# Loading two groups of an output projection's rows in five parts of unequal partition counts, in a one-core decode kernel

## The chip, the core and the metric

The kernel runs on one core of a Trainium2 chip. Its time is the device time of one execution in microseconds (us). It was run three times: 2528.84, 2529.17 and 2529.18 us, median 2529.17 us. A separate execution was profiled; the profile's times count from its first instruction.

## What is computed

One token passes through two branches that are mixed by a gate. Branch A is attention over a cache of 65,536 positions with 32 heads of 128; branch B is a small feed-forward network. All inputs are bf16.

```python
def _A_ref(x, k_cache, v_cache, wq, wo):          # x [1,1,512], caches [1,32,65536,128]
    q = (x @ wq).reshape(B, Sq, H, Dh).transpose(0, 2, 1, 3)
    scores = jnp.einsum("bhqd,bhkd->bhqk", q, k_cache) * (Dh ** -0.5)
    p = _softmax(scores, axis=-1)
    o = jnp.einsum("bhqk,bhkd->bhqd", p, v_cache)
    return o.transpose(0, 2, 1, 3).reshape(B, Sq, H * Dh) @ wo      # wo [4096,512]

def _B_ref(x, w_gate, w_up, w_down):
    return (_silu(x @ w_gate) * (x @ w_up)) @ w_down

g = _sigmoid((x * gate_w).sum(-1, keepdims=True))
return g * _A_ref(...) + (1 - g) * _B_ref(...)
```

The two caches are 512 MiB each, so the kernel reads some 1,088 MB and computes little on each byte.

## The kernel before, in words

**Tiles.** A head's 65,536 positions are cut into four tiles of 16,384 positions (G = 4). A tile is a [128 partitions x 16,384] bf16 block of 4 MB, loaded by one DMA from SyncE's queue (SP, line 112), 32 KB contiguous to a partition. There are 128 K tiles and 128 V tiles. They share a ring of five slots of 4 MB (SLOTS, lines 78 to 89): `take` draws the next free slot, `give` puts it back after the last reader.

**A K tile** is multiplied by the head's query on VectorE (line 245), halved by additions (line 249), and summed by matmuls with an identity into PSUM (`scores`, line 258); `fold` (line 272) reduces the result to one score a position. After the fourth tile of a head come the maximum (`row_max`), the exponentials (`exponentials`) and their total.

**A V tile** is multiplied by the exponentials in 32 matmuls (`values`, line 313). After a head's fourth V tile, `head_copy` and `head_turn` turn the result into a column of 128 values, and `project` (line 356) multiplies it with the head's 128 rows of wo.

**wo** comes in two ways. The first 16 heads use small tiles of four heads each (WG = 4), from a pool of two buffers (`wo_pool`, line 69), loaded by `load_wo` (line 158): one DMA of 128 partitions, four heads, 512 numbers, that is four separate rows of 1 KB to a partition, 512 KB in all. The last 16 heads' rows (`wo_late`) are loaded at the very end into a ring slot, in four pieces (`load_late`, line 163).

**The order of work** is written out by hand. Each step of the main loop (line 408) takes one K tile n and one V tile v: it issues the load of K tile n, then, at every sixteenth V tile (v = 2, 18, 34, 50), a group of wo, then the load of V tile v; after that come the vector work, the matmuls and the projection of a head that is done. All these loads are issued by SP, in this order, and a load waits until its slot's last reader is through. The built program gives each load one of eight landing semaphores in turn.

**The end.** The last three V tiles are loaded in pieces (V_CUTS, line 30), the smallest of 256 KB, then `wo_late`; then the last head is turned, 16 heads are projected, the two halves of the sum are copied (lines 459 and 460) and the output of 1 KB is stored (line 461).

Of the kernel before, what the change touches and what calls it, by code (L numbers as in the profile page):

```python
# [11 lines left out]
P = 128  # L12
# [14 lines left out]
LATE = 16  # L27
LATE_CUTS = (0, 5, 10, 14, LATE)
TURNED = 8
V_CUTS = {3: (0, 64, NB), 2: (0, 64, NB), 1: (0, 32, 64, 96, 112, NB - TURNED, NB)}  # L30


@with_exitstack
def kernel(
# [14 lines left out]
    nc = tc.nc  # L49
# [56 lines left out]
    def load(dst, cache, n, name, cuts=(0, NB)):  # L106
        h, g = divmod(n, G)
        t = take(f"{name}.{n}")
        view = t.rearrange("p (j d) -> p j d", d=Dh)
        src = cache[0, h, g * NB * P : (g + 1) * NB * P, :].rearrange("(p j) d -> p j d", j=NB)  # L110
        for a, b in zip(cuts[:-1], cuts[1:]):
            nc.sync.dma_start(out=view[:, a:b, :], in_=src[:, a:b, :])
        dst[n] = view
# [4 lines left out]
    def load_v(n):  # L118
        load(V_tiles, A_v_cache, n, "V_t", V_CUTS.get(N - n, (0, NB)))

# [35 lines left out]
    wo_tiles = {}  # L156

    def load_wo(g):
        wo_tiles[g] = wo_pool.tile([P, WG, D], bf16, name="wo_sb", tag="wo_sb")
        rows = A_wo[g * WG * P : (g + 1) * WG * P, :]  # L160
        nc.sync.dma_start(out=wo_tiles[g], in_=rows.rearrange("(h p) n -> p h n", p=P))

    def load_late(cuts):
        late = take("wo_late.0")[:, : LATE * D].rearrange("p (h n) -> p h n", n=D)
# [142 lines left out]
    def values(n):  # L307
        h, g = divmod(n, G)
        if g == 0:
            O_tiles[h] = psum_o.tile([4, 4 * Dh], f32, name="O_ps")  # L310
        end = NB if n < N - 1 else NB - TURNED
        for j in range(0, end, 4):
# [16 lines left out]
    def head_turn(h, O_sb):  # L329
        oh_ps = psum_m.tile([P, 1], f32, name="oh_ps", tag="misc")  # L330
        turned = range(NB - TURNED, NB) if h == H - 1 else ()
        for j in turned:
# [75 lines left out]
    for n, v in steps:  # L408
        if n is not None and n > G:
            load_k(n)  # L410
        if v is not None:
            if v % (WG * G) == 2 and v // (WG * G) < (H - LATE) // WG:
                load_wo(v // (WG * G))
            if v:
                load_v(v)
            if v == N - 1:
                wo_late = load_late(LATE_CUTS)
# [74 lines left out]
```

## Time and profile before

| What | Value |
|---|---|
| Median of three runs | 2529.17 us |
| Profiled execution: its own time | 2529.15 us |
| Profiled execution: span from first to last instruction | 2527.4 us |
| DMA packets, bytes | 43,019 packets, 1088.49 MB, mean 431 GB/s |
| K tiles, one load each | 128 of 4096 KB, 36.9 us from issue to landing (median) |
| V tiles in one load | 125 of 4096 KB, 29.2 us from issue to landing (median) |
| wo groups | 4 of 512 KB, 33.8 us from issue to landing (median) |
| SP issues of the wo groups | 426 to 438 ns each, first at 92.8 us, last at 1060.5 us |

The page's engines are PE (TensorE matmul), PEld (its weight loads), DVE (VectorE), ACT (ScalarE), POOL (GpSimd) and SP (SyncE, which here issues nearly all loads). L161 is line 161 of the kernel. The DMA rows give what the core's 16 DMA engines moved: a row for each queue, and a mean busy share over the 16. "instruction" queues bring program code. The time to landing runs from an issue on SP to the last of the load's 16 landing records. The chain of work is followed back from the last instruction, at each step to what released it.

### The profile page before, as it was taken

The page shows a single profiled execution, that of the slowest core. Times are in us where ns is not written, and L with a number is a line of the kernel's source. Part 1 is how long each engine was busy: PE and PEld are TensorE (multiplying, and loading weights), DVE is VectorE, ACT ScalarE, POOL GpSimd, SP SyncE. Part 2 cuts the span into 40 slices and gives each one's busy share as a digit, 9 for nine tenths or more (in the row PEclk, how much of TensorE's full clock was granted, in tenths as well). Part 3 has the DMA queues.
Part 4 walks back from the last instruction along what each step waited for, and adds up shares of the span by engine and source line. Part 5 has one row for each costly group of instructions (what it writes and reads, how often), then busy time and mean ns, then how long its engine had stood idle before and what let it go on. Part 6 is the DMA issues. An engine that isn't in the chain of part 4 may idle for free.

```text
span 2527.4 us, 13150 instructions
## 1 busy us (share of the span) xinstructions
PE 1523.3 (60%) x5770; PEld 579.9 (23%) x5770; DVE 2083.6 (82%) x744; ACT 77.6 (3%) x207; POOL 0.7 (0%) x6
## 2 busy tenths in 40 slices
PE   3666556655666555556665666566556665665568
PEld 1322222221222212212222222222222221222223
DVE  6988888788888999988888888888888888888860
ACT  1000000000000000000000000000000000000000
POOL 0000000000000000000000000000000000000000
PEclk7877777777777777787777777777877777777779
DMA  9999999999999999999999999999999999999998
GB/s 415 435 431 431 434 434 432 433 432 431 434 431 435 432 431 433 433 432 434 432 433 432 432 433 434 433 432 432 433 434 433 432 432 432 435 434 432 431 432 370
DMA packets 43019, 1088.49 MB, mean 431 GB/s; under 512 B 4689, under 2 KB 8786, under 8 KB 9170
## 3 DMA queue, kind: packets, MB, share of 16 engines
q1 hardware_dynamic: 42674, 1087.65, 99.9%
q8 instruction: 45, 0.74, 0.1%
q14 instruction: 12, 0.10, 0.0%
q10 hardware_dynamic: 288, 0.00, 0.0%
HBM read 1087.64 MB, written 0.00 MB: 430 GB/s over the span
## 4 chain that ended last, share of the span: by engine, by line
DMA 71%; PE 22%; DVE 6%; issue 0%; ACT 0%; SPq 0%; DVEq 0%
DMA V_t<-in_A_v_cache_dram 65%; PE O_ps L313 21%; DMA K_t<-in_A_k_cache_dram 6%; DVE K_t L245 3%; DVE K_t L249 2%; PE S_ps L258 1%; DMA wo_late<-in_A_wo_dram 0%; DVE S_sb L272 0%; PE oh_ps L342 0%; DVE m L278 0%; ACT P_sb L291 0%; PE a_ps L356 0%; PE mT_ps L282 0%; ACT O_sb L326 0%; DVE top L287 0%
## 5 line engine op out<-in xcount | busy, mean ns | idle before, releaser
L313 PE MATMUL O_ps<-V_t,P_sb 128*4 128x512 bf16 x4094 | 1149.9, 451 | 672.4 <-DMA V_t<-in_A_v_cache_dram 672.4
L245 DVE TENSOR_TENSOR K_t<-K_t,q_bc 128x16384 bf16<-128x16384 bf16 (+1 forms) x159 | 1117.2, 7026 | 346.0 <-DMA K_t<-in_A_k_cache_dram 346.0
L249 DVE TENSOR_TENSOR K_t<-K_t 128x8192 bf16<-128x8192 bf16 (+1 forms) x314 | 859.8, 2738 | 8.6
L313 PEld LDWEIGHTS <-P_sb 128*4 128x4 bf16 x4094 | 392.7, 97 | 1409.4 <-issue 1064.4
L258 PE MATMUL S_ps<-K_t,ident_b 128*128 128x512 bf16 x1056 | 265.3, 395 | 97.3 <-DVE K_t L249 97.1
L258 PEld LDWEIGHTS <-ident_b 128*128 128x128 bf16 x1056 | 98.6, 102 | 245.2 <-issue 156.0
L282 PE MATMUL mT_ps<-diag,ones_f 128*128 128x128 f32 x64 | 23.9, 473 | 141.3 <-ACT diag L280 141.3
L342 PE MATMUL oh_ps<-ident_f,O_sb 4*128 4x1 f32 x256 | 55.5, 334 | 74.5 <-ACT O_sb L326 74.5
L272 DVE TENSOR_REDUCE S_sb<-S_ps 128x128 f32<-128x512 f32 x128 | 87.5, 684 | 4.8 <-PE S_ps L258 4.8
L280 ACT ACTIVATE diag<-ident_f,m 128x128 f32<-128x128 f32 x32 | 12.8, 402 | 2110.1 <-DVE m L278 2110.1
L342 PEld LDWEIGHTS oh_ps<-ident_f,O_sb 4*128 4x128 f32 x256 | 52.8, 301 | 84.1 <-ACT O_sb L326 79.8
L282 PEld LDWEIGHTS mT_ps<-diag,ones_f 128*128 128x128 f32 x64 | 14.9, 289 | 158.4 <-ACT diag L280 158.4
L459 DVE CAST out_sb<-a_ps 1x256 bf16<-1x256 f32 x1 | 0.4, 411 | 58.3 <-PE a_ps L356 58.3
L291 ACT ACTIVATE P_sb<-S_sb,bias 128x512 bf16<-128x512 f32 x32 | 23.1, 722 | 1.0
L278 DVE TENSOR_REDUCE m<-S_sb 128x1 f32<-128x512 f32 x32 | 22.0, 686 | 1.1
L326 ACT ACTIVATE O_sb<-O_ps 4x512 f32<-4x512 f32 x32 | 18.3, 572 | 132.8 <-PE O_ps L313 132.8
L147 PE MATMUL qg_ps<-wq_t,X_bc 128*128 128x512 bf16 x32 | 8.8, 443 | 13.0 <-DMA wq_t<-in_A_wq_dram 13.0
L304 DVE RECIPROCAL recip<-tot_ps 128x1 f32<-128x1 f32 x32 | 5.1, 158 | 12.5 <-PE tot_ps L299 12.5
L299 PEld LDWEIGHTS tot_ps<-rowsum,ones_f 128*128 128x128 f32 x64 | 9.5, 188 | 14.0 <-issue 14.0
L299 PE MATMUL tot_ps<-rowsum,ones_f 128*128 128x1 f32 x64 | 12.2, 260 | 0.0
L349 ACT ACTIVATE oT<-oh_ps,rg 128x1 bf16<-128x1 f32 x32 | 8.4, 264 | 63.4 <-PE oh_ps L342 63.4
L287 DVE TENSOR_REDUCE top<-mT_ps 128x1 f32<-128x128 f32 x32 | 9.1, 284 | 1.0 <-PE mT_ps L282 1.0
(42 smaller groups left out, 68.9 us busy)
## 6 DMA issues: line engine op xcount, KB each, us to landing
K_t<-in_A_k_cache_dram SPq DMA_DIRECT2D x128, 4096.0 KB, 36.9
V_t<-in_A_v_cache_dram SPq DMA_DIRECT2D x125, 4096.0 KB, 29.2
V_t<-in_A_v_cache_dram SPq DMA_DIRECT2D x4, 2048.0 KB, 31.7
wq_t<-in_A_wq_dram SPq DMA_DIRECT2D x1, 4096.0 KB, 12.3
V_t<-in_A_v_cache_dram SPq DMA_DIRECT2D x3, 1024.0 KB, 32.1
wo_sb<-in_A_wo_dram SPq DMA_DIRECT2D x4, 512.0 KB, 33.8
gu_t<-in_B_w_gate_dram SPq DMA_DIRECT2D x1, 1792.0 KB, 34.3
gu_t<-in_B_w_up_dram SPq DMA_DIRECT2D x1, 1792.0 KB, 38.2
```

The costliest lines, as they stand in the source:

```text
L245: yield nc.vector.tensor_tensor(out=K, in0=K, in1=q_rep, op=ALU.mult)
L249: yield nc.vector.tensor_tensor(out=K[:, :, 0:half], in0=K[:, :, 0:half], in1=K[:, :, half : 2 * half], op=ALU.add,)
L258: nc.tensor.matmul(S, lhsT=ident_b, rhs=K_tiles[n][:, :, c : c + QUAD], start=(c == 0), stop=(c == width - QUAD),)
L272: nc.vector.tensor_reduce(out=S_tiles[h][:, g * NB : (g + 1) * NB], in_=F_tiles.pop(n), axis=AXIS.X, op=ALU.add)
L278: nc.vector.tensor_reduce(out=m, in_=S_tiles[h], axis=AXIS.X, op=ALU.max)
L280: nc.scalar.activation(out=diag, in_=ident_f, func=ACT.Copy, scale=m)
L282: nc.tensor.matmul(mT_ps, lhsT=ones_f, rhs=diag, start=True, stop=True)
L291: nc.scalar.activation(out=P_tiles[h], in_=S_tiles[h], func=ACT.Exp, bias=bias, scale=scale, accum_out=rowsum[:, h : h + 1],)
L299: nc.tensor.matmul(tot_ps, lhsT=ones_f, rhs=rowsum[:, h : h + 1], start=True, stop=True)
L313: nc.tensor.matmul(O_tiles[h], lhsT=P_tiles[h][:, g * NB + j : g * NB + j + 4], rhs=V_tiles[n][:, j : j + 4, :], start=(g == 0 and j == 0) ...
L326: nc.scalar.activation(out=O_sb, in_=O_tiles.pop(h), func=ACT.Copy)
L342: nc.tensor.matmul(oh_ps, lhsT=O_sb[:, c * Dh : (c + 1) * Dh], rhs=ident_f[0:4, c : c + 1], start=(c == 0 and not turned), stop=(c == 3),)
```

## The change

`load_wo` cuts the first two groups' load by partitions. Group 0 (heads 0 to 3) is loaded by five DMAs of 1, 3, 5, 7 and 112 partitions, group 1 (heads 4 to 7) by five of 2, 4, 4, 6 and 112; groups 2 and 3 keep their single DMA. Destination, source and bytes are the same; all are issued by SP at the same place in the order.

```diff
+WO_PARTS = {0: (1, 3, 5, 7, 112), 1: (2, 4, 4, 6, 112)}
...
     def load_wo(g):
         wo_tiles[g] = wo_pool.tile([P, WG, D], bf16, name="wo_sb", tag="wo_sb")
         rows = A_wo[g * WG * P : (g + 1) * WG * P, :]
-        nc.sync.dma_start(out=wo_tiles[g], in_=rows.rearrange("(h p) n -> p h n", p=P))
+        rows = rows.rearrange("(h p) n -> p h n", p=P)
+        at = 0
+        for n in WO_PARTS.get(g, (P,)):
+            nc.sync.dma_start(out=wo_tiles[g][at : at + n], in_=rows[at : at + n])
+            at += n
```

## The prediction, made before the changed kernel was run

> **What bounds the kernel.** I read the page's DMA rows first, then the chain of work that ended last, then the end of the span in short windows, and last the landings of single loads. From the page:
>
> ```profile
> span 2527.4 us, 13150 instructions
> ...
> PE 1523.3 (60%) x5770; PEld 579.9 (23%) x5770; DVE 2083.6 (82%) x744; ACT 77.6 (3%) x207; POOL 0.7 (0%) x6
> ...
> q1 hardware_dynamic: 42674, 1087.65, 99.9%
> q8 instruction: 45, 0.74, 0.1%
> ...
> DMA 71%; PE 22%; DVE 6%; issue 0%; ACT 0%; SPq 0%; DVEq 0%
> ```
>
> The packets of the loads fill 99.9% of the time of the 16 DMA engines, while VectorE is busy 82% and PE 60%. Nothing else can set the end unless the loads run dry. The small row below the loads matters too: 45 packets, 0.74 MB, of program code, drawn by the same engines. The question for any change to a load is therefore: which of the 16 engines finishes last, and does it get more or fewer bytes?
>
> The windows at the end of the span answer the first half. Columns: stretch, its length, busy time of PE, PEld, DVE, ACT and POOL, granted clock, busy share of the 16 DMA engines, GB/s.
>
> ```profile
> 2510.00:2512.00 2.00, 2.00 (x11) 0.77 (x10) 0.00 (x0) 0.00 (x0) 0.00 (x0) 1.00 1.02 400
> 2512.00:2514.00 2.00, 2.00 (x11) 0.82 (x10) 0.00 (x0) 0.00 (x0) 0.00 (x0) 1.00 0.87 348
> 2514.00:2516.00 2.00, 1.82 (x9) 0.61 (x8) 0.00 (x0) 0.00 (x0) 0.00 (x0) 1.00 0.58 234
> ...
> 2522.00:2524.00 2.00, 1.95 (x19) 1.38 (x17) 0.00 (x0) 0.00 (x0) 0.00 (x0) 1.00 0.26 86
> ```
>
> The share falls to 0.58 ten microseconds before the loads are over: some engines are through and others are not. The landing records say how far apart they are. Every load leaves 16 of them; those of the last piece of V (issued at 2499.0) run from 2509.76 to 2518.51, 8.75 us. Sorted, five engines lie within 0.4 us of the first, three follow at 1.1, 2.3 and 5.1, four at 7.1 to 7.3, and four at 8.5 to 8.75 us. At 22 us into the span the same spread is 0.4 us. It grows in steps: whenever a code packet is fetched (0.88 to 0.97 us each in the packet records, about every 57 us), one engine falls back by some 1.55 us and stays back. Four engines with six such steps and four with five make 44 of the 45 packets. So the kernel's end belongs to the **four engines 8.5 us behind the first**, and the chain confirms that the end hangs on the latest landing:
>
> ```profile
> 2480.05 31.11 DMA V_t<-in_A_v_cache_dram
> 2511.16 0.02 issue
> 2511.18 12.15 DMA wo_late<-in_A_wo_dram
> 2523.33 0.04 issue
> 2523.37 1.48 PE a_ps L356 x12
> 2524.86 0.02 issue
> 2524.88 0.37 ACT out_sb L460
> ```
>
> **The change, part by part.** Only the loads of wo's groups 0 and 1 change; bytes stay the same (512 KB a group, 4 KB a partition), and in the order of the built instructions nothing moves on any engine but SP, which gets eight more DMA issues.
>
> *What one partition costs an engine.* Row: the K load issued at 92.40 lands after 22.0 us, at 114.4; the wo load issued right behind it, at 92.78, after 22.8 us, at 115.6. The second pair: 388.41 + 37.2 = 425.6 and 388.79 + 38.2 = 427.0. So wo's 512 KB take 1.2 to 1.4 us, say 1.3, of every engine's time. With 128 partitions over 16 engines, eight to each, a partition costs 1.3 / 8 = 0.163 us.
>
> *What moves.* The part of 112 partitions gives each engine seven, one fewer than before. An engine that takes none of the small parts thus saves 0.163 us a group, 0.33 us over both. The 16 partitions left over go to whichever engines take the small parts: parts of at most seven partitions, one to an engine, reach at most seven engines, so at least nine get nothing of them. If the parts always begin with the same engine, that one gets four partitions more and one fewer in each group, net +3 and +3: at most 6 x 0.163 = 0.98 us later; and if each part went whole to one and the same engine, 16 + 16 - 2 = 30 partitions, 4.9 us. No load of before has fewer than 128 partitions on its inner side except the final 1 KB, so which engines take the parts is not in the trace; nor does the trace number the engines. For the four late engines the bounds are therefore -0.33 us (none takes a small part) and +0.98 us (one is the favoured engine; the 4.9 us need a whole-part engine that is also late, which I leave to the tail). I take **-0.33 us**: nine or more engines of 16 get less, and the late four behave alike (six code packets each), so they are probably neighbours, on one side of the division.
>
> [...]
>
> *The added loads' own overhead.* Nearest row: V's last pieces of 256 KB, issued at 2494.2 and 2499.0, land 0.65 us apart, against 0.60 for their share of a 4 MB load that takes 9.68 us. Thus at most 0.05 us a load on an engine; the late engines get none of the eight small ones if the choice above holds. I cost it at nothing; upper end 8 x 0.05 = 0.4 us, only for an engine that takes part in all.
>
> *SP's issues and new waits.* A wo issue takes 0.43 us, so four more are 1.7 us a group. After the first wo issue (92.78) SP next issues at 101.19, after the second (388.79) at 407.42: the gap covers them. But the program hands out eight landing semaphores in turn, and a load is not issued before the eighth load ahead of it has landed. Five loads in place of one shift this. Group 0: its fourth and fifth part wait for loads that landed at 75.6 and 85.3; behind them K moves from 103.3 to 104.7 (V's landing), V from 111.8 to 114.4 (K's landing), and K from 113.9 to about 115.5. Group 1: the fifth part waits until 396.5, K moves from 409.5 to about 416, V from 424.7 to 425.6. In these moments the engines still hold queued loads until 125.3 us (group 0) and until about 436 us (group 1), 10 and 20 us more. So these waits cost nothing; if the cover were gone, each us of lateness beyond it would cost one us. The landing itself is hidden as well: wo's rows, landed at 115.6 and 427.0, are first used by PE at 177.1 and 488.0. On PE two weight loads get two more semaphores to wait for; both have risen some 60 us before.
>
> *Sum.* The span 2527.4 - 0.33 = 2527.1 us; the profiled execution took 2529.15, 1.75 us more than its span, which gives 2528.8 us. The median of the three runs, 2529.17, is 0.02 us above that execution, so no correction is needed. What is late next: the same four engines, still over 1 us behind the next four.
>
> **The rivals.**
>
> *The small parts fall on late engines.* Same arithmetic, other side: +0.98 us at most, some +0.8 us if the favoured ones are among the late, so 2530.0 us, slower. [...] Against: only two or three engines get much more, five are nearly free. It decides once a late engine receives more than two small-part partitions in all.
>
> *Collision at the memory's doors.* With 112 partitions, an engine's seven no longer begin where its usual eight do, so two engines may write side by side into the same stretch of partitions. Price from the rows: the 112-part takes 7 x 0.163 = 1.14 us a group; if it went at half speed all along, +2.3 us in both groups, less 0.33: 2531.1 us; at half speed for a quarter of the time, +0.57 - 0.33: 2529.4. For it: nothing in the trace, where all loads have the same alignment. Against: the wo packets of 1 KB already run below the pace of a 4 MB load (1.3 us against 9.68 / 8 = 1.21), so an engine is not pressing as hard. [...]
>
> *The landing waits starve the engines.* Place: K's issue after group 1, held to about 416 by the semaphore turn. It decides only if the hold reaches past 436 us, 20 us more; a load missed outright in each group would cost 2 x 9.68, so 2548.5 us. Against: the margins above.
>
> *The change does not shift anything.* If the engines share a small part's 1 KB rows evenly, all 16 keep their load: 2529.15 us, plus up to 0.4.
>
> **How the numbers follow.** Forecast, late engines relieved, 2528.8 us: 0.55. No shift, around 2529.2: 0.17. Late engines loaded, about 2530.0: 0.13. Collision, 2529.4 to 2531.1: 0.10. Starved, 2548.5: 0.02. Something that gains more than I can derive, such as a code packet moved to another engine: 0.03. The range: below, the forecast less 0.6, since the runs of before differ by 0.34 among themselves and the lag is read from one execution; above, the collision's bound, rounded: 2528.2 to 2531.2. A measurement of this kernel tells about 0.2%, 5.1 us, from no change; nearly every case lies inside it: same 0.96, slower 0.03 (starved, or whole parts on one late engine with collision), faster 0.01.
>
> **What would show it right or wrong.** In the page after, wo's issues appear as loads of 4 to 28 KB and two of 448 KB, and the DMA rows keep their bytes and 99.9%. If the forecast holds, the windows before the end show the engines idling less early (share above 0.58 between 2514 and 2516) because the early engines have more to do, and the chain's last wo landing moves from 2523.3 to about 2523.0. If the parts fell on late engines, that landing moves back, to about 2524.2. A DMA share below 0.98 near 115 to 130 or 416 to 440 us would mean starvation. The forecast is wrong if the lag between first and last landing grows, or if the code packets, not these partitions, change place.

## The result, and the profile after

The changed kernel takes **2531.98 us** in the median of 18 executions, against 2529.08 us for the kernel before in its 18: 2.90 us or 0.115% slower. The ratio of the means is 1.002, with a 95% interval from 1.0012 to 1.0028; it lies above the ratio of the medians because three of the 18 executions took 2538.9, 2540.9 and 2554.0 us, where the 18 of before lie between 2528.8 and 2529.4. All 18 of the changed kernel, from 2531.4 up, lie above all 18 of before. Ratios here leave out executions more than 1.5% above the fastest of their kernel, which concerns two executions of e9 alone. The forecast was 2528.8 us, in a range up to 2531.2: the time lies outside it, and on the other side.

The profiled execution (2531.86 us) stands for the median. Its page first: span, the queue that carries the loads, the code queue, and the shares of the chain that ended last.

```profile
span 2530.1 us, 13160 instructions
...
q1 hardware_dynamic: 42709, 1087.65, 99.9%
q8 instruction: 45, 0.74, 0.1%
...
DMA 72%; PE 21%; DVE 6%; issue 0%; SPq 0%; ACT 0%; DVEq 0%
```

Bytes, code packets and the 99.9% are those of before; the engines are as busy as ever and yet 2.7 us later. The loads' queue has 35 packets more, all of them under 512 bytes (4,689 such packets before, 4,724 after). They are landing records: a load of 128 partitions leaves 16 of them, each load of 112 still leaves 16, and the small parts leave four for the load of one partition, then 3, 5, 7, 2, 4, 4 and 6. That is 35. Read as one record from each engine that took part, a small part ran on as many engines as it has partitions (and one partition, four rows, on four).

Where do 2.7 us come from when busy shares don't change? From the rate. These are the 40 us around each of the two groups (columns: stretch, length, busy time of PE, PEld, DVE, ACT, POOL, granted clock, DMA share, GB/s), before:

```profile
100.00:140.00 40.00, 22.97 (x96) 8.51 (x94) 33.69 (x11) 0.00 (x0) 0.00 (x0) 0.86 1.01 432
410.00:450.00 40.00, 20.96 (x80) 7.42 (x80) 32.11 (x11) 0.00 (x0) 0.00 (x0) 0.79 1.01 431
```

and after:

```profile
100.00:140.00 40.00, 22.39 (x92) 8.24 (x91) 31.55 (x11) 0.00 (x0) 0.00 (x0) 0.83 1.02 418
410.00:450.00 40.00, 22.30 (x82) 7.71 (x81) 30.20 (x11) 0.00 (x0) 0.00 (x0) 0.74 1.01 415
```

The share stays at 1.01 or above and the rate falls: the packets occupy the engines longer for the same bytes. 14/432 of 40 us are 1.3 us, 16/431 are 1.5 us; together 2.8 us, the whole difference, as near as such a rate can be read: it counts whole packets, and e1 and e7 below, with the same cut, read 414 and 418 in the first stretch, 0.4 us apart. In the stretches away from the two groups the rates of the two kernels agree (432 and 434 GB/s from 1260 to 1340 us). In the packet records of the first stretch, wo's 1 KB packets carry 0.46 us more per engine than at their usual 46 ns, and the 32 KB packets beside them 1.1 us more, nearly all of it in the V tile that follows: its first packets take up to 2.08 us instead of 1.21, 14 of them 1.87 or more. In the second stretch it is 0.62 and 1.05 us. The four add up to 3.2 us, somewhat more than the span has lost; packets of one engine overlap a little there (the share is above 1).

The end, in the windows and the chain that the prediction showed of before:

```profile
2510.00:2512.00 2.00, 1.29 (x7) 0.42 (x5) 0.00 (x0) 0.00 (x0) 0.00 (x0) 1.00 0.98 410
2512.00:2514.00 2.00, 2.00 (x11) 0.76 (x9) 0.00 (x0) 0.00 (x0) 0.00 (x0) 1.00 1.05 420
2514.00:2516.00 2.00, 2.00 (x11) 0.81 (x10) 0.00 (x0) 0.00 (x0) 0.00 (x0) 1.00 0.73 295
```

```profile
2478.22 33.16 DMA V_t<-in_A_v_cache_dram
2511.38 0.02 issue
2511.40 4.08 SPq L172
2515.47 0.04 issue
2515.52 10.51 DMA wo_late<-in_A_wo_dram
2526.03 0.04 issue
2526.07 1.49 PE a_ps L361 x12
```

The chain has one link more, SP's issue of a piece of `wo_late` (L172), and still ends on the same landing: that has moved from 2523.3 to 2526.0, and everything behind it with it.

### The profile page after: what moved, and what is told of

Read it like the earlier page. It is cut to its first block, busy times and chain, and to the rows that moved or that the text cites. A ratio compares the mean times of both kernels' runs of the same rounds, so it can differ in the third digit from the quotient of the medians.

```text
span 2530.1 us, 13160 instructions
## 1 busy us (share of the span) xinstructions
PE 1521.5 (60%) x5770; PEld 579.5 (23%) x5770; DVE 2083.4 (82%) x744; ACT 77.6 (3%) x207; POOL 0.7 (0%) x6
## 2 busy tenths in 40 slices
DMA packets 43054, 1088.49 MB, mean 430 GB/s; under 512 B 4724, under 2 KB 8821, under 8 KB 9205
## 3 DMA queue, kind: packets, MB, share of 16 engines
q1 hardware_dynamic: 42709, 1087.65, 99.9%
## 4 chain that ended last, share of the span: by engine, by line
DMA 72%; PE 21%; DVE 6%; issue 0%; SPq 0%; ACT 0%; DVEq 0%
DMA V_t<-in_A_v_cache_dram 63%; PE O_ps L318 20%; DMA K_t<-in_A_k_cache_dram 9%; DVE K_t L250 3%; DVE K_t L254 2%; PE S_ps L263 1%; DMA wo_late<-in_A_wo_dram 0%; DVE S_sb L277 0%; PE b_ps L229 0%; DVE m L283 0%; SPq L172 0%; PE oh_ps L347 0%; ACT P_sb L296 0%; PE a_ps L361 0%; PE mT_ps L287 0%
```

## The experiments

The theory after the first look: **a load that covers only part of the partitions makes engines write where other engines write, and two of them there share one door's pace** (collision; "door" is this theory's word for a way into the core's memory that a set of partitions is supposed to share; no trace shows one). Its rivals: each added load costs something by itself (count); the small parts crowd a few engines (small parts). Each kernel below is the kernel before with only the named edit, and was timed beside the kernel before on the same chip. In the cuts of code, `...` marks what is left out, and a run named behind `#` is the one whose line it is.

| Kernel | Median us | Before | Ratio, 95% interval |
|---|---|---|---|
| e1 16 + 112 | 2532.58 | 2529.03 | 1.0022, 1.0007 to 1.0037 |
| e2 by head | 2529.16 | 2529.03 | 1.0000, 0.9991 to 1.0010 |
| e3 small extra | 2529.25 | 2529.03 | 1.0001, 0.9992 to 1.0010 |
| e4 V halves | 2544.06 | 2529.03 | 1.0060, 1.0043 to 1.0076 |
| e5 wo halves | 2532.94 | 2529.04 | 1.0015, 1.0006 to 1.0024 |
| e6 wo even/odd | 2529.05 | 2529.04 | 1.0000, 0.9991 to 1.0009 |
| e7 16 + 112, all groups | 2537.77 | 2529.04 | 1.0035, 1.0021 to 1.0049 |
| e8 by head, all groups | 2529.50 | 2529.04 | 1.0002, 0.9993 to 1.0011 |
| e9 aligned shift | 2536.22 | 2529.07 | 1.0025, 1.0012 to 1.0039 |
| e10 every fourth | 2529.23 | 2529.07 | 1.0001, 0.9992 to 1.0010 |
| e11 quarters | 2534.20 | 2529.07 | 1.0020, 1.0011 to 1.0029 |
| e12 V even/odd | 2529.07 | 2529.07 | 1.0000, 0.9991 to 1.0009 |
| f1 aligned, even | 2538.49 | 2529.08 | 1.0044, 1.0019 to 1.0068 |
| f2 shift, late groups | 2532.29 | 2529.08 | 1.0020, 1.0009 to 1.0030 |
| f3 group 0 alone | 2530.67 | 2529.08 | 1.0006, 0.9997 to 1.0015 |
| f4 group 1 alone | 2530.49 | 2529.08 | 1.0005, 0.9997 to 1.0014 |
| f5 large first | 2529.82 | 2529.07 | 1.0007, 0.9998 to 1.0016 |
| f6 extra by eights | 2530.62 | 2529.07 | 1.0011, 1.0002 to 1.0020 |

The intervals reach 2 us and more to either side, too wide to tell a difference of 1.5 us. Where the text reads smaller ones, it goes by the executions: all 11 of f3 and all 11 of f4 lie above all 32 of before on their chip (from 2530.0 and 2530.4, against at most 2529.7).

**e1: the 112 partitions without the uneven parts.**

```diff
-WO_PARTS = {0: (1, 3, 5, 7, 112), 1: (2, 4, 4, 6, 112)}
+WO_PARTS = {0: (16, 112), 1: (16, 112)}
```

> Groups 0 and 1 of wo in two parts, 16 and 112 partitions: no engine gets more or fewer rows than another (one partition of the small part each), but the 112 partitions still give each engine seven instead of eight. Collision theory (engines with seven partitions write into each other's stretches of partitions): the loss stays, 1.4 + 1.6 us in the stretches 112 to 118 and 424 to 430 us, and without the 0.33 us saved: about 2532.1 us. Count theory (each of the eight added loads costs some 0.37 us): two added loads, about 2529.8 us. Small-part theory (the parts of 1 to 7 partitions crowd a few engines): no loss, 2529.1 us.

Measured: 3.55 us over before, with two added loads instead of eight and none of fewer than 16 partitions. The rate from 100 to 140 us and from 410 to 450 us:

```profile
100.00:140.00 40.00, 24.83 (x100) 9.08 (x99) 31.90 (x11) 0.00 (x0) 0.00 (x0) 0.83 1.02 414
410.00:450.00 40.00, 22.14 (x82) 7.60 (x81) 30.45 (x10) 0.00 (x0) 0.00 (x0) 0.74 1.01 412
```

The loss is 18/432 and 19/431 of 40 us, 1.7 and 1.8 us. Neither eight added loads nor parts of a few partitions are needed. One of the ten executions took 2551.8 us.

**e2: as many loads, none displaced.**

```diff
...
+        cuts = ((0, 1, 0, D), (1, 2, 0, D), (2, 3, 0, D), (3, 4, 0, D // 2), (3, 4, D // 2, D))
+        for h0, h1, c0, c1 in cuts if g < 2 else ((0, WG, 0, D),):
+            nc.sync.dma_start(out=wo_tiles[g][:, h0:h1, c0:c1], in_=rows[:, h0:h1, c0:c1])
```

> Groups 0 and 1 of wo in five loads each again, but cut by heads and columns, each over all 128 partitions (the last head in two halves of 512 bytes a row). Collision theory: nothing is displaced, 2529.1 to 2529.5 us (the halved rows may cost a little). Count theory: as many loads as in the changed kernel, about 2532 us. Small-part theory: 2529.1 us.

Measured: 0.13 us over before. Where wo lands the rate is nearly before's, which reads 437 and 434 GB/s in these two windows (the changed kernel 350 and 289):

```profile
112.00:118.00 6.00, 1.79 (x8) 0.66 (x7) 4.14 (x4) 0.00 (x0) 0.00 (x0) 1.00 1.07 437
424.00:430.00 6.00, 2.46 (x11) 0.85 (x10) 4.07 (x1) 0.00 (x0) 0.00 (x0) 0.93 1.05 428
```

The count theory falls. The same cut in all four groups, with 16 added loads, is e8:

> All four groups of wo in five loads over all 128 partitions, cut by heads and columns. Collision theory: 2529.1 to 2529.4 us and no execution far above the rest. If the turn of the landing semaphores makes single executions late, some lie 7 to 22 us above.

Measured: 0.46 us, 0.03 us a load, and all 11 executions within 0.5 us of each other. The changed turn of the landing semaphores made none of these 11 late, which speaks against it as the cause of late executions; with 3 late of 18 in the changed kernel it is no proof.

**e3: the small parts alone**, ahead of before's full loads.

```diff
+SMALL = {0: (1, 3, 5, 7), 1: (2, 4, 4, 6)}
...
+        for n in SMALL.get(g, ()):
+            nc.sync.dma_start(out=spare[at : at + n, g], in_=rows[at : at + n])
+            at += n
+        nc.sync.dma_start(out=wo_tiles[g], in_=rows)
```

> Before's single loads of 128 partitions are kept, and the eight small parts are loaded in addition, into a spare tile on partitions 0 to 15 that nothing reads (128 KB more in all). Collision theory in its narrow form (only the displaced 112 partitions collide): small loss, at most some 0.5 us, 2529.1 to 2529.7 us. Count theory: 2532 us. Small-part theory: 2532 us. If favoured engines are the late ones, the small parts alone add up to 1.1 us.

Measured: 0.22 us for 128 KB more (which take 0.3 us at 432 GB/s). The small parts by themselves are not the cause, and the engines that they load are not the late ones, or the end would have moved by up to 1 us. The landings of V's last piece show where they went: sorted from the first engine to the last, the last four lie 8.66 to 8.94 us behind the first (before 8.55 to 8.75), while the fourth to the eighth have moved back by 0.5 to 1.5 us.

**e4 and e12: the same question on a tile of 4 MB.** V tile 60 is cut into its lower and upper 64 partitions (e4), or into the even and the odd ones (e12).

```diff
+V_PARTS = {60: ((0, 64), (64, P))}         # e4
+V_PARTS = {60: ((0, 2), (1, 2))}           # e12: first, step
...
+                nc.sync.dma_start(out=view[p0:p1, a:b, :], in_=src[p0:p1, a:b, :])               # e4
+                nc.sync.dma_start(out=view[p0:P:step, a:b, :], in_=src[p0:P:step, a:b, :])       # e12
```

> One V tile of 4 MB (tile 60) is loaded as partitions 0 to 63 and 64 to 127, two loads of 2 MB; wo as before. [...] Count theory: one added load, 2529.5 us. Small-part theory: 2529.1 us.

> V tile 60 in two loads of 2 MB, the even and the odd partitions, against the lower and the upper half (2544.06 us). Collision theory: every engine stays in its stretch, 2529.05 us, no halved rate between 1280 and 1308 us. If any cut of the tile by partitions is harmful: 2544 us.

Measured: 15.03 us and 0.00 us over before. The windows at the tile, of e4:

```profile
1260.00:1276.00 16.00, 7.50 (x33) 2.72 (x31) 12.82 (x4) 0.00 (x0) 0.00 (x0) 0.81 1.01 434
1280.00:1306.00 26.00, 9.00 (x39) 4.61 (x37) 17.93 (x11) 2.16 (x6) 0.00 (x0) 0.70 1.02 214
1312.00:1330.00 18.00, 10.13 (x43) 3.77 (x42) 10.00 (x2) 0.00 (x0) 0.00 (x0) 0.78 1.00 431
```

and of e12 in the middle one:

```profile
1280.00:1306.00 26.00, 18.40 (x76) 8.11 (x75) 20.45 (x12) 2.16 (x6) 0.00 (x0) 0.80 1.00 433
```

Half the partitions in a block gave half the rate, 214 GB/s against 434 just before, at a mean busy share of 1.02 over the 16 engines. Every second partition gave the full 433. So it is not the number of partitions or of loads but which partitions a load covers. The slow stretch lasts about 29 us, though, not the 19.4 of the tile at half speed (twice its 9.68, so 9.7 us more): 182 packets of 32 KB take over 2 us, and the tile has only 128, so what follows it is slowed as well. Why by half as much again is open.

**e5, e6, e10, e11: blocks and steps on wo.** Groups 0 and 1 as two halves, as even and odd partitions, as every fourth partition, as four blocks of 32.

```diff
+WO_PARTS = {0: (64, 64), 1: (64, 64)}       # e5
+        for at, step in ((0, 2), (1, 2)) if g < 2 else ((0, 1),):         # e6
+            nc.sync.dma_start(out=wo_tiles[g][at::step], in_=rows[at::step])
+WO_LISTS = ((0, 4, 32), (1, 4, 32), (2, 4, 32), (3, 4, 32))       # e10: first, step, count
+WO_LISTS = ((0, 1, 32), (32, 1, 32), (64, 1, 32), (96, 1, 32))    # e11
```

> Groups 0 and 1 of wo as partitions 0 to 63 and 64 to 127, two loads each, no engine with more rows than another. If the doors belong to stretches of partitions and a load over half the partitions reaches half of them, as the V tile in halves showed (rate 205 to 229 GB/s), each group's 1.3 us become 2.6 us or, with the same after-effect as there (14.9 us lost for 9.7), up to 3.3 us: 2531.6 to 2533.0 us, and 112 to 118 us falls well below 437 GB/s. If only the odd count of 112 is harmful: 2529.1 us.

> Groups 0 and 1 of wo as the even and the odd partitions, two loads of 64 partitions each. Both loads reach all stretches. If an engine keeps its usual stretch with every second partition of it, nothing collides: 2529.1 us. If the engine is given four listed partitions in a row and these lie in two doors, pairs collide part of the time: about 2530 to 2532 us. If any load of fewer than 128 partitions is harmful whatever its place: as the halves, about 2532 us.

> Groups 0 and 1 of wo in four loads of 32 partitions each, every fourth partition. If each of the 16 engines owns a stretch of eight partitions in a row, it writes two of its own each time: 2529.0 to 2529.2 us, no fall of the rate between 112 and 118 us. [...]

> Groups 0 and 1 of wo in four loads of 32 neighbouring partitions. Doors of eight partitions: each load reaches 4 of 16, a quarter of the rate, so 4 x 1.2 - 1.2 = 3.6 us lost a group, 2536 us, with after-effect up to 2538 us. [...] Number of loads: as the four loads of every fourth partition.

Measured: blocks 3.90 and 5.13 us, steps 0.01 and 0.16 us. The rate from 112 to 118 us is 262 GB/s in e5 and e11 (the line of e5 first), and in e6 what it is before, 437:

```profile
112.00:118.00 6.00, 1.77 (x8) 0.65 (x7) 2.18 (x4) 0.00 (x0) 0.00 (x0) 1.00 1.03 262
112.00:118.00 6.00, 1.89 (x8) 0.75 (x8) 4.83 (x5) 0.00 (x0) 0.00 (x0) 0.88 1.06 437
```

Blocks of 32 cost far less than the 7.2 us forecast for doors eight partitions wide; they lie nearer to the blocks of 64, 1.2 us above them, with executions from 2532.8 to 2535.8. Which partitions an engine takes is not in the trace, so I can't say by which rule the shares of such a load stay clear of each other; that an engine keeps a stretch of eight neighbouring partitions, as the expectations have it, is an assumption of mine.

What these runs show is that blocks of partitions cost time and steps don't, at the same counts. That two engines meet at one door is the reading that fits them, and it is argued, not seen. One rival has no run of its own: in every cut the partitions written and the rows read from the chip's memory change together, so the reading side could be what is slow. Against it stands e2, where each load read within one stretch of 128 KB and lost nothing, while e5's loads read four stretches of 64 KB and lost 2 us each group.

**e7, f3, f4: does the loss add up?** e7 has 16 + 112 in all four groups; f3 and f4 the change on one group each.

```diff
+WO_PARTS = {g: (16, 112) for g in range(4)}    # e7
+WO_PARTS = {0: (1, 3, 5, 7, 112)}              # f3
+WO_PARTS = {1: (2, 4, 4, 6, 112)}              # f4
```

> All four groups of wo in parts of 16 and 112 partitions. Collision theory: the loss of the run with two groups (3.55 us) doubles: 2536.1 us. If it belongs to the early part of the program or to the first such loads alone: 2532.6 us. Single executions 7 to 22 us above the rest were seen only in kernels with a part of 112 partitions (4 of 28); if the collisions cause them, they come here at least as often; if the changed turn of the landing semaphores causes them, they come in the kernel cut by heads as well.

> The change on group 0 alone (1, 3, 5, 7, 112). Collision theory: its share of the loss, read from the rate as 1.4 to 1.5 us, less half of any relief: about 2530.5 us. If single late executions come from group 0, where engines run closest together: some 7 to 22 us above, as in 3 of 18 of the changed kernel.

> The change on group 1 alone (2, 4, 4, 6, 112). Collision theory: 1.6 us lost, about 2530.6 us; with group 0's alone the two losses add up to the change's 2.9 us. Late executions: none if they belong to group 0 and its close engines, otherwise as in the changed kernel.

f3 loses 1.59 us and f4 1.41: together 3.00, against the change's 2.90. Neither has a late execution in 11, so that these come from group 0, as one expectation had it, is not borne out. e7 loses 8.73 us where twice e1 would be 7.1: if its first two groups cost what they do in e1, the two later ones cost 2.6 us each instead of 1.8.

**e9, f1, f2, f5, f6: a shift without displacement, and a second effect.** e9 was to move rows off seven of the 16 engines while most engines stay where they are (both by my assumption of how partitions are dealt out, which no trace shows); if that had gained, it would have beaten both kernels. `WO_LISTS` gives first partition, step and count of each load.

```diff
+WO_LISTS = ((7, 8, 7), (63, 8, 9), (3, 8, 16), (1, 4, 32), (0, 2, 64))    # e9; f2: groups 2, 3
+WO_LISTS = ((7, 8, 16), (3, 8, 16), (1, 4, 32), (0, 2, 64))               # f1
+WO_LISTS = ((0, 2, 64), (1, 4, 32), (3, 8, 16), (7, 8, 16))               # f5
+        for at, step, n in ((7, 8, 16), (3, 8, 16)) if g < 2 else ():              # f6, into a spare tile
...
```

> The change's shift of rows with as little displacement as possible: groups 0 and 1 of wo in five loads by steps of 2, 4 and 8 partitions (64, 32 and 16 partitions, every engine in its usual stretch of eight) and the last 16 partitions (7, 15, 23, ... 127) as loads of 7 and 9. Seven of the 16 engines save one partition a group, as in the change. If engine time limits and the late engines are among those relieved: 2529.05 - 0.33 = 2528.7 us. If the door of a stretch limits, nothing is saved, since each door carries the same bytes: 2529.0 to 2529.3 us. If the loss comes from uneven loads as such: about 2532 us.

It gained nothing (its fastest of 12 executions took 2529.52 us). Ten executions spread up to 2547.9 us, with a median of 2533.65; two more took 2598.0 and 2601.3 us. Its profile shows something that no theory of mine had:

```profile
112.00:118.00 6.00, 1.89 (x8) 0.75 (x8) 4.52 (x5) 0.00 (x0) 0.00 (x0) 0.86 1.05 393
118.00:130.00 12.00, 3.32 (x8) 0.97 (x8) 11.93 (x3) 0.00 (x0) 0.00 (x0) 0.50 0.96 372
130.00:160.00 30.00, 18.54 (x73) 6.57 (x71) 17.32 (x7) 0.00 (x0) 0.00 (x0) 0.77 1.03 399
160.00:198.00 38.00, 19.72 (x77) 8.35 (x77) 32.84 (x15) 2.16 (x6) 0.00 (x0) 0.73 1.00 386
200.00:230.00 30.00, 12.80 (x51) 4.46 (x49) 24.20 (x5) 0.00 (x0) 0.00 (x0) 0.76 1.01 437
```

From wo's landing to 199 us nearly every 32 KB packet of all 16 engines takes 1.36 us instead of 1.21, though wo is long in, and it stops where a code packet is fetched (199.0 us; the one fetched at 135.7 did not stop it). That costs some 9 us. The next four tried to find what sets it off:

> As the run with the shifted rows, but its loads of 7 and 9 partitions are one load of 16 (every eighth partition from 7): every engine stays in its stretch and all get the same. If the uneven, displaced loads set off the stretch of 388 GB/s: 2529.0 to 2529.4 us, all executions within 0.5 us of each other, no 32 KB packet series at 1.36 us. If loads with a step, or of 16 partitions, set it off: again a median several us above and a spread of tens of us.

> The run with the shifted rows, with the same loads for groups 2 and 3 (issued near 700 and 1060 us) instead of 0 and 1. If the slow stretch needs engines that run side by side (first to last landing 0.4 us apart, two of them 1.6 us, at group 0; 3.2 to 4.4 us at groups 2 and 3): 2529 to 2530 us with little spread. If the loads alone set it off: median and spread as in the early groups, 2529.5 to 2601 us.

> The four loads of f1 (64, 32, 16 and 16 partitions by steps of 2, 4, 8 and 8, every engine in its stretch), the large ones first. If the order sets off the slow stretch (small loads ahead of large ones): 2529.0 to 2529.4 us without spread. If loads of 16 partitions by steps of 8 do so wherever they stand: a median some us above and a spread of 10 us or more.

> Before's single loads of 128 partitions are kept; ahead of them, in groups 0 and 1, two loads of 16 partitions by steps of 8 (from 7 and from 3) go into a spare tile that nothing reads (256 KB more in all, some 0.6 us). If such loads alone set off the slow stretch: a median some us above and a spread of 10 us or more. If it takes the other step loads too: 2529.5 to 2529.9 us without spread.

f1, whose loads are all of 16, 32 or 64 partitions, is as erratic (2529.6 to 2558.2 us): the loads of 7 and 9 are not needed. Its profile (2532.88 us) shows the stretch too: from 115 us the 32 KB packets take 1.43 us, until a code packet is fetched at 136.6, and 1.21 us after it. f2 spreads from 2529.7 to 2542.0 in the later groups: it is milder there, so engines close together aren't needed either (at these groups their landings lie 3.2 to 4.4 us apart in the kernel before). f5, with the large loads first, spreads from 2529.4 to 2535.9. f6 has one execution of 12 at 2544.1 and the rest between 2530.1 and 2532.2; its median is 1.55 us over before, of which its 256 KB more take 0.6 at 432 GB/s. f2 and f5 fall between their two forecasts.

Loads of 16 partitions or fewer are in all the kernels with far-out executions, ahead of larger loads in all but f5, the mildest (the change's three late executions, and e1's one, may belong here too). Loads of 32 or 64 partitions show less: e5, e6 and e10 have no execution above 2533.5 us, though e11, with loads of 32, spreads over 2.9 us. But e3, e7, f3 and f4 have loads of 16 partitions or fewer as well, and no late execution in 10, 5, 11 and 11. **What sets the slow stretch off, and whether the change's three late executions are the same thing, stays open**; none of those three was caught in a profile.

## Why the prediction was wrong, step by step

- **What bounds the kernel**: right. DMA stays at 99.9%, the chain ends on a landing of `wo_late`, and a loss in the rate moves the end with it (2.8 us in the rate, 2.7 in the span).
- **What one partition costs, how many engines a part takes**: right as far as it can be seen. The 35 landing records, read as one from each engine, put the small parts on two to seven engines each, so the rival that the change shifts nothing (0.17) is out; the 0.163 us a partition was not measured by itself.
- **-0.33 us for the late engines**: at most a small part of the sum. Two of the signs named for it can't decide. The busy share between 2514 and 2516 us rose from 0.58 to 0.73, as forecast, but a stream that ends 2.7 us later gives that by itself. The lag from first to last landing of V's last piece did not grow: 8.75 us before, 8.65 after, 9.03 in e1, whose parts of 16 and 112 were to relieve no engine. Kernels without any relief or loss scatter as far, though (8.94 in e3, 9.07 in e2). e1 is 0.65 us slower than the change, but its part of 16 differs in other ways too, and e9, meant as the purer shift, shows no gain. Whether the 0.33 us exist isn't shown, nor which engines took the small parts.
- **Favoured engines are late ones** (0.13): refuted by e3, whose small parts moved other engines back and left the last four nearly where they were.
- **The loads' own overhead at nothing**: right; 0.03 us a load (e8).
- **SP's issues and landing waits at nothing**: right, and nearly to the time. The waits came where they were worked out; most are a little later because the landings themselves are:

```profile
100.42 0.35 SPq L113 DMA_DIRECT2D V_t<-in_A_v_cache_dram  x1
104.53 0.35 SPq L113 DMA_DIRECT2D K_t<-in_A_k_cache_dram  x1
115.46 0.33 SPq L113 DMA_DIRECT2D V_t<-in_A_v_cache_dram  x1
115.89 0.37 SPq L113 DMA_DIRECT2D K_t<-in_A_k_cache_dram  x1
```

  Forecast for the last three: 104.7, 114.4, 115.5. In group 1 K went out at 417.3 (forecast 416) and V at 428.5 (425.6). The DMA share over the 40 us of each group is 1.02 and 1.01, as before: nothing starved. (Windows of 2 and 4 us dip to 0.88 and 0.91, but the kernel before dips to 0.93 and 0.92 in the same ones.)
- **The step that failed is the collision**: the forecast's sum put the cost of cutting the loads into blocks of partitions at nothing, and held the collision as a rival at 0.10 with 2529.4 to 2531.1 us. The cutting cost 2.8 us in the rate. Two errors in it. Its chance: I counted "nothing in the trace" against it, though a trace in which every load covers 128 partitions can't speak for or against, and I took the 8% between 1 KB and 32 KB packets for slack. Its bound: I let only wo's own 1.14 us a group go at half speed. No row of before shows that speed, it was an assumption; e4 measured 214 GB/s of 434 for blocks of 64 partitions, and the change 350 and 289 of 437 and 434 where its parts land. The runs show that the load behind pays more than wo does (1.1 of 1.55 us per engine in the first group); e4 shows the same at 4 MB, 15 us where the tile alone explains 9.7. A reading that fits is that some engines are back at their places while others still write there; no trace shows who writes where. With the load behind counted in, at what it paid here, the bound would have been 2 × (1.14 + 1.1) = 4.5 us instead of 2.3, and the range would have held the time.

## What to carry to other kernels

In a stream that keeps all DMA engines full, cut a load by rows or columns that every partition has (0.03 us a load here), or by a step of two or four partitions (0.01 and 0.16 us for two loads of 512 KB), not into blocks of partitions: 112 of 128 cost 1.4 to 1.8 us a load of 512 KB, halves 2 us, and a 4 MB tile in halves 15 us. (That blocks cost and steps of two and four don't is shown here; that doors are the reason is the reading that fits.) Evening out engines by a few KB is not worth that: the whole relief to be had was 0.33 us by the prediction's estimate. And when a rival has no row for or against it, bound it by what lies behind it in the queue as well, and leave it more than one chance in ten.

## What the runs showed of the hardware that was not expected

- All 16 DMA engines ran slower at one common pace without being idle (busy share 0.96 to 1.07 in windows of 12 us and more): in e9 at 1.36 us a 32 KB packet instead of 1.21 (388 GB/s instead of 432) from 115 to 199 us, in f1 at 1.43 us from 115 to 136.6. Both stretches began behind loads of which the first had 16 partitions or fewer, and ended at a code packet.
- The same block cut cost more later in the program: by e7, 2.6 us a group near 740 and 1090 us against 1.8 near 114 and 427 us in e1. In the kernel before, the engines' landings lie 1.5 to 1.7 us apart at the first two groups and 3.2 to 4.4 at the later two; whether that is the reason isn't shown.
- A code packet of 16 KB, 0.88 to 0.97 us long in the kernel before, puts the engine that fetches it back by about 1.4 to 1.6 us, and that engine stays behind to the end: two engines with one fetch each lie 1.56 and 1.61 us behind the first at 93 us, and after 44 fetches the last four engines lie 8.55 to 8.75 us behind it.
